# A fused retention and squared-ReLU kernel: q of the first pairs in 2 KB rows, one score task per pair, clusters joined one group earlier, and a re-drawn plan

## The chip, the cores and the metric

The kernel runs on one core of a Trainium2 chip. The time is that of the device for one execution, in microseconds (us); the number to compare is the median of ten executions. One further execution was recorded by the hardware profiler, and everything that is read from a profile comes from that one. The engines are named as in the profile: PE (matmul) with its weight loads PEld, DVE (vector), ACT (scalar), POOL (GpSimd) and SP (the queue that issues most DMAs).

## The reference

```python
scores = (1 / sqrt(D)) * q @ k.T                      # per batch (8) and head (8), 576 positions, D = 64
Dmat[h, i, j] = gamma[h] ** (i - j) if i >= j else 0  # gamma = 1 - 2 ** (-5 - h)
attn = (scores * Dmat) @ v
x = attn with the heads side by side                  # 4608 rows of 512
h = x @ w_in                                          # 512 -> 2048
out = relu(h) ** 2 @ w_out                            # 2048 -> 512
```

Inputs and output are float32; the kernel computes in float16 with float32 sums.

## The kernel before

**Units and groups.** A unit is 128 positions of one batch with all eight heads (or the last 64 positions of two batches, a "tail"). There are 36 units, and two units make a group, 18 groups in all. For each group PE does the retention part in small 64x64 matmuls (four at a time in the corners of the array, the helper `quad`, L357): `psc` are the scores, `psS` the sums of k times v that carry the state on, `psO` the outputs from masked scores and from the state. DVE masks the scores (`rx` L490, `rT` L692), updates the state (`R`, `Rm`, `stmp`) and writes the group's input to the feed-forward part (`xT`, L577 and L751). Then PE does the first product `ph` (L876, 64 matmuls of 128x256 per group), ACT takes the ReLU (`rl`, L884), ACT or DVE the square (`gT`, L894 and L896), and the second product `po` follows: for group 0 directly (L916, 32 matmuls of 128x512), for the others by Strassen's seven products (L973), with sums of `gT` on DVE (`gS`, L946) and differences of `w_out` on DVE (`wT`, L827).

**The first eight units** are loaded in pairs: one DMA each for k, q and v of 256 positions (L316, 512 KB, packets of 512 bytes because two neighbouring positions of one head lie side by side). The casts to float16 are `kx`, `qx` (L424) and `vx` (L420); PE turns k and q around (`psT`, L439), and ACT or DVE copies the turned tiles out (`kqT`, L450). In these four groups the scores are two tasks, one for the even and one for the odd positions (`fs`, L479), each with two banks of PSUM and a lock of its own (`prS`, `prO`). All later units are loaded one by one (k L301, q L298, v L301), cast on POOL (L371, L382, L387) and turned by a DMA (`kqT`, L400).

**Clusters.** A change from the large matmuls to the small ones and back costs PE time, so small tasks are put together. From group JOIN = 5 on, the outputs from the state of group g and the scores of group g+1 are one task (`f1`, L790), and the sums of g+1 and the rest of the outputs of g another (`f2`, L794). Before that, a group's scores and sums are one task (`fa`, L778) and its outputs one with a drain in the middle (`fb`, L809).

**What sets the order.** The program order on every engine comes from a list planner in the kernel (`Schedule`, L16): every task has an engine, a key, an assumed duration and its dependences. `emit` walks through time with these durations and writes the tasks out in the order in which they would start. The assumed durations and the landing delays (`LAG`, `after=`) thus change no instruction, only the order. The queues are in order: what waits at the head of SP or POOL holds up everything behind it.

**The head.** 34 `warm` matmuls (L256) fill PE while the first data come. POOL makes masks and issues the eight casting weight DMAs (w_in 0 to 3 and w_out 0 to 3, L331, numbered w0 to w7 below); the first of them waits for the landing of v of the first pair, and k of the third pair waits for w5 (`behind`). A small constant for the tails (`iota_pt` on POOL L272 and L273, `vdl_tail` on DVE L182, `vdec_tail` on ACT L184) is made here too.

Of the kernel before, what the change touches and what calls it, by code (L numbers as in the profile page):

```python
# [9 lines left out]
FP32 = mybir.dt.float32  # L10
# [5 lines left out]
class Schedule:  # L16
# [7 lines left out]
    def add(self, eng, key, dur, fn, deps=(), acq=(), after=None, lag=0.0):  # L24
        t = dict(eng=eng, key=key, dur=dur, fn=fn, acq=acq, n=len(self.tasks), users=[], free=[], lag=lag,
                 left=len(deps), ready=0.0, lat=self.LAT[eng] if after is None else after)
        for d in deps:
            d["users"].append(t)
        self.tasks.append(t)
        return t  # L30
# [11 lines left out]
    def emit(self):  # L42
# [13 lines left out]
        now = 0.0  # L56
        while True:
            for e in ready:
                if busy[e]:
                    continue  # L60
                held = []
                while ready[e]:
                    item = heapq.heappop(ready[e])
                    t = item[2]
                    if all(self.count[r] >= t["acq"].count(r) for r in t["acq"]):
                        for r in t["acq"]:
                            self.count[r] -= 1
                        t["start"] = now
                        order.append(t)
                        busy[e] = True  # L70
                        push(now + t["dur"], "end", t)
                        break
                    held.append(item)
                for item in held:
                    heapq.heappush(ready[e], item)
            if not events:
                break
            now = events[0][0]
            while events and events[0][0] <= now + 1e-9:
                _, _, what, t = heapq.heappop(events)  # L80
                if what == "end":
                    busy[t["eng"]] = False
                    for w in t["users"]:

                        push(now + (0.0 if w["eng"] == t["eng"] else t["lat"]), "dep", w)
                    for g in t["free"]:
                        push(now + t["lat"], "free", g)
                elif what == "dep":
                    t["left"] -= 1
                    if t["left"] == 0:  # L90
                        push(now + t["lag"], "go", t)
                elif what == "go":
                    heapq.heappush(ready[t["eng"]], (t["key"], t["n"], t))
                else:
                    t["left"] -= 1
                    if t["left"] == 0:
                        self.count[t["res"]] += 1
# [6 lines left out]
def kernel(  # L104
# [9 lines left out]
    nc = tc.nc  # L114
# [96 lines left out]
    mask2 = const.tile([P, 2, 2, 64], FP32, name="mask2")  # L211
    nc.gpsimd.memset(mask2, 1.0)
    for c in range(2):
        for e in range(2):
            m = mask2[c * 64:(c + 1) * 64, e]
            nc.gpsimd.affine_select(out=m, in_=m, compare_op=ALU.is_ge, fill=0.0, base=-e, pattern=[[1, 2], [2, 64]],  # L216
                                    channel_multiplier=-2)
# [12 lines left out]
    BESIDE = 1.1  # L230
# [5 lines left out]
    JOIN = 5  # L236
    LAG = {"k4": 0.7, "q4": 0.5}
# [37 lines left out]
    tail_pool = add_gated("POOL", 4, "v", 2.2, make_tail_pool)  # L275
    tail_dec = add("DVE", 0, 0.3, lambda: make_vdec("tail", tile_of["iota_pt"]), deps=[tail_pool])
# [31 lines left out]
    def add_load_pair(name, u):  # L308
        n = "kqv".index(name)

        def fn():
# [4 lines left out]
            t = nc.sync.dma_start(out=x, in_=(k, q, v)[n][b, :, c * P:(c + 2) * P, :].rearrange("h (p e) d -> p h (e d)", e=2))  # L316
# [3 lines left out]
        loaded[name, u] = loaded[name, u + 1] = dma_task(0, 1.81 if loaded else 2.9, fn, acq=("wst",) if name != "q" else (),  # L320
# [4 lines left out]
    def add_weight(i):  # L325
# [10 lines left out]
        t = add("SP", 0, 2.75, lambda: None, deps=last_load + [issue], after=2.1 + LAG.get(f"w{i}", 0.0))  # L336
# [25 lines left out]
    def half(x):  # L362
        return slice(64 * x, 64 * x + 64)
# [39 lines left out]
    def add_unit_pair(u, base):  # L403
# [4 lines left out]
        for i, name in enumerate("kqv"):  # L408
            xs[name] = []
            for e in range(2):  # L410
                eng = ("DVE" if (e if name == "v" else lead) else "ACT" if name == "k" and u >= 4 or u == 2 and e else
                       "DVE" if name == "q" and u == 2 else "POOL")

                def fc(name=name, e=e, eng=eng):
# [4 lines left out]
                    if name == "v":  # L419
                        (nc.vector if eng == "DVE" else nc.gpsimd).tensor_tensor(  # L420
                            out=t.rearrange("p (h d) -> p h d", d=D), in0=x,
                            in1=vdec[f"pair{e}"].rearrange("p (h o) -> p h o", o=1).to_broadcast([P, H, D]), op=ALU.mult)
                    else:
# [10 lines left out]
        for i, name in enumerate("kq"):  # L434
# [9 lines left out]
            for s in range(2):  # L444
                on_act = i == 0 or s == 0 or u > 0

                def fe(i=i, s=s, on_act=on_act):
                    if i == 0:
                        tile_of["kqT", u + s] = work.tile([P, 2 * NP, P], FP16, name="kqT", tag="kqT", bufs=6)
                    (nc.scalar.copy if on_act else nc.vector.tensor_copy)(  # L450
                        out=tile_of["kqT", u + s][:, i * NP:(i + 1) * NP].rearrange("p x (e t) -> p e x t", e=2),
                        in_=tile_of["psT", u, i][:, :, :, half(s)])
# [15 lines left out]
    def add_ret_pair(g):  # L468
# [7 lines left out]
        for e in range(2):  # L476
            tag = "prS" if e == 0 else "prO"

            def fs(e=e, tag=tag):  # L479
# [6 lines left out]
            t = add("PE", base + 3 + e, 0.4, fs, deps=T["kqT", u] + T["kqT", u + 1], acq=(tag, "kq", "ff", "ff"))  # L486
            ms = []
            for a in range(2):
                def fm(e=e, a=a):
                    nc.vector.tensor_tensor(  # L490
                        out=rT[e][:, a], in0=rT["ps", e][a].rearrange("p (n i) -> p n i", i=P),
                        in1=mask2[:, e].rearrange("p (o e) i -> p o (e i)", o=1).to_broadcast([P, NP, P]), op=ALU.mult)
                ms.append(add("DVE", base + 5 + e, 0.66, fm, deps=[t] + ms))
                sched.free("ff", ms[-1:])
            sched.free(tag, ms)
            masked += ms
# [67 lines left out]
        t = add("PE", base + 23.9, 0.6, fo1, deps=masked + T["kvx", u], acq=("prO", "ff", "ff"))  # L564
# [8 lines left out]
        for s in range(2):  # L573
            def fx(s=s):
                if s == 0:
                    tile_of["x", g] = x_pool.tile([P, NP, 2 * P], FP16, name="xT", tag="xT")
                nc.vector.tensor_tensor(  # L577
                    out=tile_of["x", g][:, :, s * P:(s + 1) * P].rearrange("p n (i e) -> p n e i", e=2),
                    in0=tile_of["psO", g][s].rearrange("p (n e i) -> p n e i", n=NP, e=2),
                    in1=gam_f.rearrange("p n (i e) -> p n e i", e=2), op=ALU.mult)  # L580
            T["x", u + s] = add("DVE", base + 25 + s, 0.7, fx, deps=[t] + ([T["x", u]] if s else []), acq=() if s else ("x",))
            sched.free("ff", [T["x", u + s]])
        sched.free("prO", [T["x", u + 1]])
# [117 lines left out]
    def after_sums(g, t, key, res):  # L701
# [24 lines left out]
        r2 = add("DVE", key + 0.3, 0.65, fr2, deps=[r1], acq=("R",))  # L726
# [95 lines left out]
    def add_wT(i, in0, in1):  # L822
        ts = []
        for h in range(2):
# [3 lines left out]
            ts.append(add("DVE", WT_KEY + i, 0.7, f, deps=sum((wcast[j] for j in range(4, 8 if i else 6)), [])))  # L828
# [6 lines left out]
    for x, y in ((t2, t1), (t4, t2)):  # L835
        for p in y:
            for w in x:
                sched.need(w, p)
# [19 lines left out]
    def add_ff(g):  # L858
# [10 lines left out]
        for fb in range(NF // nf):  # L869
# [18 lines left out]
            def fg(fb=fb, on_act=on_act):  # L888
# [6 lines left out]
                else:  # L895
                    nc.vector.tensor_tensor(out=t, in0=rl, in1=rl, op=ALU.mult)  # L896
            r = add("ACT", place(4 * fb + 4), 0.6, fr, deps=[f1[-1]], acq=("rl",))
            sched.free("ff", [r])
            sq.append(add("ACT" if on_act else "DVE", place(4 * fb + 6), 0.63 if on_act else 0.55, fg, deps=[r] + sq[:1],
                          acq=() if fb else ("g",)))  # L900
# [31 lines left out]
    def add_strassen(g, us, base, sq):  # L932
# [7 lines left out]
        def add_sum(k, key, parts, in0, in1, op, deps, start=()):  # L940
            out_ = []
            for h in range(parts):
# [4 lines left out]
                out_.append(add("DVE", key + h, (BESIDE if h else 0.5) if parts > 1 else 0.8, f, deps=deps(h, parts) + list(start)))  # L947
# [164 lines left out]
```

## Time and profile before

| what | value |
|---|---|
| median of 10 executions (lowest, highest) | 289.84 us (289.27, 290.74) |
| the profiled execution: its own time | 289.79 us |
| its span, from first to last instruction | 288.1 us |
| PE busy | 281.2 us, 98% of the span |
| ACT, DVE, POOL busy | 187.6, 178.1, 87.4 us |
| mean granted PE clock | 1.00 |
| HBM read, written | 36.70 MB, 9.44 MB |

The profiled execution's time is 1.69 us longer than its span. A busy PE is not proof that PE works at its peak, since matmuls overlap; the step from one start to the next tells more. In the timeline the start of a group is in the first column and its length in the second; what ended the idle time before it stands in brackets. The chain of waits follows the last instruction back to what released it.

### The profile page before, as it was taken

The numbers are of one execution on the slowest core, as the hardware profiler recorded it, in microseconds if no ns is written. First come the engines' busy times: TensorE is split into PE (matmuls) and PEld (weight loads), VectorE is DVE, ScalarE is ACT, GpSimd is POOL, SyncE is SP. The second block draws the span as 40 slices with busy tenths as digits, with TensorE's granted clock in tenths as the row PEclk, the third lists the DMA queues.
The fourth block names the chain that finished last, engine by engine and source line by source line (L and its number), as shares of the span: only waits on it lengthen the run. The fifth ranks groups of instructions, "written<-read, shape, count | busy, mean of one in ns | idle before, by whom it ended". The sixth has DMA issues, their size and how long they took to land.

```text
span 288.1 us, 10135 instructions
## 1 busy us (share of the span) xinstructions
PE 281.2 (98%) x4346; PEld 236.1 (82%) x4346; DVE 178.1 (62%) x341; ACT 187.6 (65%) x363; POOL 87.4 (30%) x124
## 2 busy tenths in 40 slices
PE   7999999999999999999999999999999999999994
PEld 2568767888888888888888888888888888888883
DVE  3772389768466756548767574676666566364632
ACT  5558975667584857657576748675848675847830
POOL 5660036443524242434335433362432000000000
PEclk9999999999999999999999999999999999999999
DMA  7999999999999898999999897989989020102004
GB/s 200 276 208 207 248 288 284 149 246 165 224 212 164 221 211 204 193 201 179 226 170 234 193 206 187 251 192 250 163 215 191 0 77 2 73 2 75 0 4 144
DMA packets 122156, 49.94 MB, mean 173 GB/s; under 512 B 94720, under 2 KB 117760, under 8 KB 122112
## 3 DMA queue, kind: packets, MB, share of 16 engines
q1 hardware_dynamic: 117568, 44.84, 71.8%
q0 software_dynamic: 4224, 4.19, 8.8%
q8 instruction: 34, 0.56, 0.8%
q10 hardware_dynamic: 320, 0.26, 0.4%
q14 instruction: 10, 0.08, 0.1%
HBM read 36.70 MB, written 9.44 MB: 160 GB/s over the span
## 4 chain that ended last, share of the span: by engine, by line
PE 89%; DMA 3%; DVE 2%; POOL 2%; issue 2%; DVEq 0%; POOLq 0%
PE ph L876 44%; PE po L973 36%; PE psO L357 4%; DMA w_in<-in_moe_w_in_dram 3%; PE po L916 2%; PE psS L357 2%; PE psc L357 2%; DVE rx L490 1%; DVE o L996 0%; POOL mask L216 0%; DVE gS L946 0%; POOL vx L420 0%; POOL w_in L331 0%; PE psT L439 0%; DVE R L461 0%
## 5 line engine op out<-in xcount | busy, mean ns | idle before, releaser
L876 PE MATMUL ph<-xT,w_in 128*128 128x256 f16 x1152 | 136.6, 273 | 0.1
L876 PEld LDWEIGHTS <-w_in 128*128 128x128 f16 x1152 | 111.4, 98 | 14.5 <-DMA w_in<-in_moe_w_in_dram 0.4
L884 ACT ACTIVATE rl<-ph 128x512 f16<-128x512 f32 x144 | 84.3, 587 | 50.2 <-PE ph L876 47.6
L894 ACT ACTIVATE gT<-rl 128x512 f16<-128x512 f16 x118 | 74.4, 631 | 3.4
L973 PEld LDWEIGHTS <-gS 128*128 128x128 f16 x544 | 51.7, 98 | 6.6 <-DVE gS L946 0.2
L973 PE MATMUL po<-wT,gS 128*128 128x256 f16 x408 | 55.8, 273 | 0.0
L973 PEld LDWEIGHTS <-gT 128*128 128x128 f16 x408 | 39.6, 98 | 4.7
L946 DVE TENSOR_TENSOR gS<-gT,gS 128x512 f16<-128x512 f16 (+1 forms) x51 | 29.9, 586 | 21.1 <-ACT gT L894 20.4
L973 PE MATMUL po<-w_out,gT 128*128 128x256 f16 x272 | 36.7, 273 | 0.0
L387 POOL TENSOR_TENSOR v<-v,vdec_full 128x512 f16<-128x512 f32 x24 | 25.9, 1077 | 18.1 <-DMA v<-in_v_dram 16.1
L371 POOL CAST kq<-k 128x512 f16<-128x512 f32 x28 | 19.6, 699 | 36.0 <-DMA k<-in_k_dram 33.4
L946 DVE TENSOR_TENSOR gS<-gT 128x1024 f16<-128x1024 f16 x34 | 26.1, 768 | 6.5 <-ACT gT L894 6.3
L382 POOL CAST kq<-q 128x512 f16<-128x512 f32 x24 | 16.1, 671 | 36.7 <-DMA q<-in_q_dram 36.5
L896 DVE TENSOR_TENSOR gT<-rl 128x512 f16<-128x512 f16 x26 | 11.8, 453 | 21.2 <-ACT rl L884 21.2
L996 DVE TENSOR_TENSOR o<-po,u 128x256 f32<-128x256 f32 x33 | 13.9, 422 | 15.5 <-PE po L973 7.8
L986 ACT COPY u<-po 128x256 f32<-128x256 f32 x34 | 12.5, 368 | 15.6 <-PE po L973 15.5
L751 DVE TENSOR_TENSOR xT<-psO,gam_full 128x512 f16<-128x512 f32 x28 | 18.0, 685 | 4.2 <-PE psO L357 4.1
L996 DVE TENSOR_TENSOR o<-po,p 128x256 f32<-128x256 f32 x18 | 7.6, 424 | 20.6 <-ACT u L986 12.5
L973 PE MATMUL po<-w_out,gS 128*128 128x256 f16 x136 | 18.0, 273 | 0.0
L692 DVE TENSOR_TENSOR rT<-psc,mask_full 128x512 f16<-128x512 f32 x24 | 15.6, 683 | 3.5 <-PE psc L357 3.2
L973 PE MATMUL po<-wT,gT 128*128 128x256 f16 x136 | 17.6, 273 | 0.0
L461 DVE TENSOR_TENSOR R<-stmp,dec 128x512 f16<-128x512 f32 (+1 forms) x18 | 13.3, 741 | 0.5
(82 smaller groups left out, 221.4 us busy)
## 6 DMA issues: line engine op xcount, KB each, us to landing
out_dram<-o SPq DMA_DIRECT2D x32, 256.0 KB, 2.5
k<-in_k_dram SPq DMA_DIRECT2D x24, 256.0 KB, 4.4
q<-in_q_dram SPq DMA_DIRECT2D x96, 64.0 KB, 3.1
v<-in_v_dram SPq DMA_DIRECT2D x24, 256.0 KB, 3.8
pair<-in_k_dram SPq DMA_DIRECT2D x4, 512.0 KB, 4.2
pair<-in_q_dram SPq DMA_DIRECT2D x4, 512.0 KB, 7.5
pair<-in_v_dram SPq DMA_DIRECT2D x4, 512.0 KB, 7.3
w_in<-in_moe_w_in_dram POOLq DMA_DIRECT2D x4, 512.0 KB, 9.0
```

The costliest lines, as they stand in the source:

```text
L357: t = nc.tensor.matmul(out_, lhsT=lhsT, rhs=rhs, start=start, stop=True, skip_group_check=True, tile_position=(64 * row, 64 * col))
L371: op(out=out_.rearrange("p (n b a d) -> p n b a d", n=2, b=2, a=2), in_=in_.rearrange("p (a n b) d -> p n b a d", n=2, a=2))
L382: nc.gpsimd.tensor_copy(out=tile_of["kq", u][:, 1].rearrange("p (t a d) -> p a t d", t=4, a=2), in_=tile_of["q32", u].rearrange("p (a t) d ...
L387: nc.gpsimd.tensor_tensor(out=t, in0=tile_of["v32", u], in1=vdec[kind].rearrange("p (h o) -> p h o", o=1).to_broadcast([P, H, D]), op=ALU. ...
L692: tile_of["masking", g] = nc.vector.tensor_tensor(out=tile_of["rT", g][:, :, a], in0=tile_of["psc", g][a].rearrange("p (s n i) -> p s n i" ...
L751: nc.vector.tensor_tensor(out=tile_of["x", g].rearrange("p n (s e i) -> p e (n s) i", s=n, e=2)[:, c], in0=y.rearrange("p (o t r) -> p o r ...
L876: nc.tensor.matmul(tile_of["ph", g, fb][:, j, :], lhsT=w_in16[:, m, fi * P:(fi + 1) * P], rhs=tile_of["x", g][:, m, :], start=(m == 0), st ...
L884: nc.scalar.activation(out=t, in_=tile_of["ph", g, fb], func=ACTF.Relu)
L894: nc.scalar.activation(out=t, in_=rl, func=ACTF.Square)
L946: nc.vector.tensor_tensor(out=tile_of["S", g][:, k, sl], in0=in0(sl), in1=in1(sl), op=op)
L973: nc.tensor.matmul(tile_of["pb", g, bank], lhsT=left(i), rhs=right[:, i, :], start=(start and i == 0), stop=(i == HF - 1), skip_group_chec ...
L996: nc.vector.tensor_tensor(out=o_tile(u)[:, half * HM:(half + 1) * HM], in0=bank(x), in1=tile_of[name, g], op=ALU.add)
```

## The change

1. q of a pair comes in two DMAs of 128 rows of 2 KB (eight positions of one head to a row) instead of one of 1024 rows of 512 bytes. The masks (`mask2`), the casts of q, the copies of turned q and the `xT` writes follow the new order of positions.
2. The tail constant is three tasks, on POOL, DVE and ACT, beside the middle of the kernel instead of the head.
3. The scores of a pair are one task with four banks; the locks `prS` and `prO` are gone from the pairs.
4. JOIN is 4.
5. The casts of k and q of the second pair are all on ACT.
6. The planner's figures: landing delays of the early loads, 2.58 for a weight DMA with 3.0 to its landing, durations of some DVE tasks, a model in which some DVE tasks (`soft`) run at 0.22 of their speed while POOL is busy, earlier keys for group 1 (`HURRY`), and a half of `wT` waits only for the weights and the half that it reads.

```diff
-            t = nc.sync.dma_start(out=x, in_=(k, q, v)[n][b, :, c * P:(c + 2) * P, :].rearrange("h (p e) d -> p h (e d)", e=2))
+            src = (k, q, v)[n][b, :, c * P:(c + 2) * P, :]
+            if name == "q":
+                for a in range(2):
+                    t = nc.sync.dma_start(out=x[:, NP * a:NP * a + NP].rearrange("p t d -> p (t d)"),
+                                          in_=src.rearrange("(a x) (r t) d -> a r x (t d)", a=2, t=8)[a])
+            else:
+                t = nc.sync.dma_start(out=x, in_=src.rearrange("h (p e) d -> p h (e d)", e=2))
...
-    mask2 = const.tile([P, 2, 2, 64], FP32, name="mask2")
+    mask2 = const.tile([P, 2, 8, 16], FP32, name="mask2")
...
+                    elif name == "q":
+                        x = tile_of["q32", u].rearrange("p (a t) (s d) -> p a (t s) d", a=2, s=2)[:, :, NP * e:NP * e + NP]
+                        engines[eng](out=t.rearrange("p (t a d) -> p a t d", t=NP, a=2), in_=x)
...
+                    if i == 0:
+                        out_, in_ = out_.rearrange("p x (e t) -> p e x t", e=2), in_[:, :, :, half(s)]
+                    else:
+                        out_ = out_.rearrange("p x (t r) -> p t x r", r=16)
+                        in_ = in_.rearrange("p e y (r x) -> p (e y) x r", x=NP)[:, :, :, 16 * s:16 * s + 16]
...
-                eng = ("DVE" if (e if name == "v" else lead) else "ACT" if name == "k" and u >= 4 or u == 2 and e else
-                       "DVE" if name == "q" and u == 2 else "POOL")
+                eng = ("DVE" if (e if name == "v" else lead) else "ACT" if name == "k" and u >= 4 or u == 2 and name != "v" else "POOL")
...
-        for e in range(2):
-            tag = "prS" if e == 0 else "prO"
-
-            def fs(e=e, tag=tag):
+        def fs():
+            for e in range(2):
                 ps = rT["ps", e] = banks("psc")
...
-            t = add("PE", base + 3 + e, 0.4, fs, deps=T["kqT", u] + T["kqT", u + 1], acq=(tag, "kq", "ff", "ff"))
+        t = add("PE", base + 3, 0.8, fs, deps=T["kqT", u] + T["kqT", u + 1], acq=("kq", "kq", "ff", "ff", "ff", "ff"))
...
-    JOIN = 5
-    LAG = {"k4": 0.7, "q4": 0.5}
+    JOIN = 4
+    LAG = {"k0": 0.3, "q0": 0.6, "v0": 0.3, "k2": 0.2, "q2": 0.5, "v2": 1.0, "w2": 0.7, "w7": 1.4, "k4": 0.3, "q4": 1.1, "v4": 0.9, "q6": 0.8, "v6": 0.2}
...
-    tail_pool = add_gated("POOL", 4, "v", 2.2, make_tail_pool)
-    tail_dec = add("DVE", 0, 0.3, lambda: make_vdec("tail", tile_of["iota_pt"]), deps=[tail_pool])
+    tail_pool = add_gated("POOL", 10, "v", 0.45, make_tail_pool)
+    tail_log = add("DVE", 3 * L, 0.25, make_tail_log, deps=[tail_pool])
+    tail_dec = add("ACT", 3 * L, 0.3, make_tail_dec, deps=[tail_log], after=0.2)
...
-        t = add("SP", 0, 2.75, lambda: None, deps=last_load + [issue], after=2.1 + LAG.get(f"w{i}", 0.0))
+        t = add("SP", 0, 2.58, lambda: None, deps=last_load + [issue], after=3.0 + LAG.get(f"w{i}", 0.0))
...
-            ts.append(add("DVE", WT_KEY + i, 0.7, f, deps=sum((wcast[j] for j in range(4, 8 if i else 6)), [])))
+            ts.append(add("DVE", WT_KEY + i, 0.68, f, deps=wcast[4 + h] + (wcast[6 + h] if i else []), soft=True))
```

Positions of the tasks in the changed program, engine by engine: PE executes the same 4346 matmuls. The 34 warm ones stand in portions of 12, 3, 6, 2, 6, 2, 1, 1, 1 instead of 11, 3, 4, 3, 5, 2, 2, 4. On SP, k and q of unit 8 and k of unit 9 stand ahead of the first and second store, and the two stores of group 1 stand behind k of unit 11.

## Prediction

> **What bounds the kernel now.** I read the page first: busy times and slices.
>
> ```profile
> span 288.1 us, 10135 instructions
> ...
> PE 281.2 (98%) x4346; PEld 236.1 (82%) x4346; DVE 178.1 (62%) x341; ACT 187.6 (65%) x363; POOL 87.4 (30%) x124
> ...
> PE   7999999999999999999999999999999999999994
> ```
>
> PE is busy nearly everywhere, and no other engine passes 65%. To see if this is real work I took the table of windows and the PE timeline, step by step from one matmul's start to the next.
>
> ```profile
> 62.00:260.00 198.00, 197.81 (x3304) 173.04 (x3304) 126.77 (x217) 130.98 (x254) 62.22 (x77) 1.00 0.82 171
> ```
>
> Between 62 and 260 us PE lacks 0.2 us. From the first `ph` at 17.74 to the end the 1152 `ph` and 952 `po` of 256 columns go at 0.109 us a step and the 32 wide `po` at 0.216: 2104 x 0.1092 + 32 x 0.216 = 236.7 us that no order can change. The last PE step ends at 283.96, so 266.2 - 236.7 = 29.5 us is small matmuls, transposes and changes between them, and only one plain wait is in it: w1, below. So time can be won in three places: before the first `ph`, in that wait, and in the clusters of small matmuls. What follows the last matmul (to 288.1) keeps its instructions.
>
> The head, from the timeline and, last two lines, the chain of waits:
>
> ```profile
> 5.88 0.76 DVE L424 CAST kx<-pair 128x512 f16<-128x512 f32 x2
> 6.36 0.73 PE L439 MATMUL psT<-ident,kx 128*128 128x128 f16 x8 [0.31 <-DVE kx L424]
> ...
> 17.74 3.51 PE L876 MATMUL ph<-xT,w_in 128*128 128x256 f16 x28
> ...
> 19.76 1.21 PEld L876 LDWEIGHTS <-w_in 128*128 128x128 f16 x12 [0.38 <-DMA w_in<-in_moe_w_in_dram]
> ```
>
> ```profile
> 11.02 8.71 DMA w_in<-in_moe_w_in_dram
> 19.77 1.49 PE ph L876 x12
> ```
>
> The chain goes through the landing of w1 (19.72), not through the 17.74: PE starts on w0, then waits 0.38 us for w1. The semaphore updates give the landings: k0 5.06, q0 6.86, v0 8.66, k2 10.47, q2 12.29, v2 14.01, w0 17.29, w1 19.72, w2 22.22, w3 24.88, w4 27.42, w5 30.47, w6 32.56, w7 35.41. It is one string: 1.8 us a pair load, about 2.6 us a weight, with the DMA engines full.
>
> **The change, part by part.**
>
> *q in 2 KB rows.* A pair load is 1024 packets of 512 B, 64 on each of 16 engines at 32 ns: 1.8 us by the landings. 2 KB packets to SBUF do not occur; the nearest row is the stores, whose 2 KB packets take a median 84 ns (mean 90 to 101 beside other traffic), against 4 x 32 = 128 ns for the same bytes. That gives 16 x 90 = 1.4 us, 0.4 to 0.45 saved for each q; bounds zero (if the time goes by bytes) and 0.6 (84/128 of 1.8). Two q loads stand ahead of w1: it lands 0.9 earlier at best; 0.4 if w0 follows only its issue, which waits for v0 (issue 8.96) and so for one q; nothing if rows do not matter. I take 0.6: w1 at 19.1. The cut in two adds one SP issue per pair (a q issue took 0.56 us at the start); the string hides it.
>
> The Trainium skill, "DMA: Bandwidth & Descriptors", Specifications, says that 512 B already suffices for line rate, and its Rules for kernel authors say that two transfers to disjoint partition halves are not worth it against one; by these the gain here would be zero. The trace's 512 B packets move 251 to 267 GB/s and its 2 KB ones 325 to 364, so I weigh the row higher.
>
> *Does PE follow?* The changed order on PE, with the durations above: 12 warm end where kx now ends a wait (6.36), so the earlier kx (DVE no longer waits until 5.75 for the tail constant, k0 landed 5.06) gives nothing there. psT k, 3 warm, psT q end at 8.03 as before; 6 warm to 9.4; psc to 10.2; psS waits for POOL's vx (w0 issue 0.99 after v0 at 8.2, then 1.04): 10.65 to 11.05; 2 warm; psT of k2 at 11.5 (k2 at 10.0, two ACT casts of 0.62), 6 warm, psT of q2 at 13.25; 2 warm; psO (1.07) to 15.2; 1 warm; psc (0.72; its kqT is ready at 15.0) to 16.2; psS 0.4; 1 warm: first `ph` at 17.0 instead of 17.74, with xT at 16.6 and w0 at about 16.7. 16 `ph` take 1.75, so PE meets w1 at 18.75 and waits 0.35. After 32 `ph` and psO it stands at 19.15 + 1.75 + 1.09 = 22.0; before, the same work (28 `ph`, psO, 4 `ph`) ended at 22.7. Start: 0.7 won. But in the new order 92 `ph` and not 100 stand ahead of the po that needs w5: PE comes there at 29.4 and w5, shifted by 0.6, lands at 29.9. Before, PE came at 31.0 with w5 at 30.47. This leaves 31.0 - 0.87 - 29.9 = 0.2, or 0.7 if w5 follows w4 by the usual 2.55 and not by 3.05. **I take 0.45**, bounds 0 and 0.9.
>
> *The copies of turned q* get a stride of four in PSUM, which no row shows: bounds 425 ns (DVE, L450) and 0.69 (the DVE tasks that read float32 from PSUM); ACT's copies took 586 to 603 in the shapes that occur. The 0.26 between falls only on one copy ahead of psc, and PE waits for POOL's vx there. Casts of q: shape of L382, 0.67 against 0.69 on POOL. `xT` with a strided read: L751 has such a read and takes 685. All zero. The casts of the second pair add 2 x 0.62 to ACT, idle there since 8.81, and take 0.42 and 0.63 from DVE and POOL.
>
> *Tail constant*: 0.41 on POOL, 0.23 on DVE, 0.30 on ACT move to about 60 us, where DVE and ACT have a third free; its reader is group 8. Zero; 0.3 if an `rl` stood on the path.
>
> *One score task per pair.* By start times on PE, the small clusters of groups 2 and 3 (without psT) now last 0.38 + 0.57 + 1.36 + 0.62 + 0.52 + 1.09 = 4.54 (psS 43.05, psc 44.19, psO with half a psc 47.51, psS 49.19, second half 50.57, psO 55.56). Whole tasks: psc 0.57 to 0.72, psS 0.38, psO 1.07, psS 0.38, psc 0.57 to 0.72, psO 1.09: 4.06 to 4.36. **0.35 won**; bounds 0 (the waits inside come back as waits for DVE's masks) and 0.48. Four banks of eight at once is a new constraint; PE's other tasks then have four.
>
> *JOIN 4.* From the chain of waits:
>
> ```profile
> 62.06 0.38 PE psc L357 x32
> 62.44 0.29 PE psS L357 x32
> ...
> 67.64 0.24 PE psO L357 x8
> 67.88 0.09 issue
> 67.96 0.57 PE psO L357 x39
> ...
> 85.57 0.25 PE psO L357 x16
> 85.82 0.26 PE psc L357 x32
> ...
> 89.67 0.38 PE psS L357 x32
> 90.05 0.40 PE psO L357 x48
> ```
>
> Groups 4 and 5 pay 0.67 (scores, sums), 0.89 (outputs, with the drain) and 0.66 (76.94, scores of 5). Joined, as at 85.57 and 89.67, it is 0.67 + 0.51 + 0.78. **0.26 won**, rounded 0.3, and this one hangs on nothing but the order. The whole order has 39 clusters instead of 40.
>
> The plan's figures and the `wT` dependences add no instruction; they show only in the order.
>
> **Sum:** 0.45 + 0.35 + 0.3 = 1.1; 289.79 - 1.1 = **288.7 us**. The profiled execution is 0.05 under the median, so I use it as it stands. All bounds at their best: 0.9 + 0.48 + 0.3 = 1.7, 288.1. If this holds: 288.1 to 289.2.
>
> **Rivals.**
>
> *A: the loads do not keep up with the earlier scores (slower).* With JOIN 4 the scores of group 5 come 80 large matmuls behind those of group 4 and not 112: at 61.25 + 0.67 + 8.8 = 70.75, where they were at 76.94. They need the transpose of unit 11:
>
> ```profile
> 67.35 1.48 SPq L400 DMA_TRANSPOSE kqT<-kq  x1
> ```
>
> It landed at 72.39. If SP is not earlier, PE stands 1.65 us; if k of unit 9, which now waits for an earlier landing on SP's ring of eight, is 1 us later still, 2.65. Then 288.7 + 1.65 to 2.65 = 290.4 to 291.4. Against it: k of unit 8 was issued at 42.15 behind a store that waited for ACT, and is now ahead of it, at 39.8 by v of unit 6 (40.35, released by POOL's qx, which comes 0.95 earlier); 25.2 us of issues later this puts the transpose at 65.0 and its landing at 70.0. The slack is 0.7. It decides from a landing later than 72.4.
>
> *B: rows do not matter and the gain at the start is lost*, because w1 and w5 land when they did: 0.3 + 0.35 = 0.65, and if the score task's banks make PE wait as well, 0.3 alone: 289.1 to 289.5.
>
> *C: the order merely deals the waits anew*, PE meeting k4, q4 and vx just before 50 us (each computed with 0.1 to 0.4 us of slack) and losing 1.1 there: 289.8, no change.
>
> **Chances.** Below 0.2% (0.58 us) a measurement of this kernel can hardly tell from no change. Forecast 0.58; the better half of B (289.1 to 289.2) 0.10; its rest and C, 289.3 to 290.4, 0.15; A 0.17. Faster 0.68, same 0.15, slower 0.17. Range 287.9 to 290.4: the forecast's bounds with 0.2 for the spread between executions, and up to the foot of A.
>
> **What would show it.** First `ph` near 17.0; w1 near 19.1 (if 19.7, rows do not matter); PE idle before the po of w5 under 0.5; clusters of groups 2 and 3 summing to 4.1 to 4.4 and the two joined ones of group 4 to 0.51 and 0.78; no wait of PE for a transpose near 70. Wrong if PE's timeline has a gap of over 0.5 us behind 20 us.

## The result and the profile after

The changed kernel is **slower**: a median of 291.36 us (289.63 to 293.34, 15 executions) against 289.77 us for the kernel before (289.27 to 290.74, 51 executions). The ratio is 1.0057, with a 95% interval of 1.0045 to 1.0069. It also varies more: its executions spread over 3.7 us, those before over 1.5 (beside the experiments below, in 19 to 30 executions each, over 2.1 to 5.2). Ratios leave out executions more than 1.5% above the fastest of their kernel (one of twelve in e1, three of twelve in e13, two of thirty of the kernel before beside e9 to e12), while medians and spreads leave out none.

The profiled execution took 292.53 us, so it is one of the long ones. From its page, busy times and slices (PEclk is the granted PE clock in tenths):

```profile
span 290.8 us, 10142 instructions
...
PE 282.2 (97%) x4346; PEld 237.4 (82%) x4346; DVE 177.3 (61%) x340; ACT 188.5 (65%) x365; POOL 87.1 (30%) x123
...
PE   8999999969999999999999999999999999999994
...
PEclk9999999997999999999999999999999999999999
```

PE still dominates, but its ninth slice (58 to 65 us) has fallen to 6, and in the tenth the clock is at 7. The table of windows (start and end, length, PE, PEld, DVE, ACT and POOL busy, clock, DMA share, GB/s) shows it finer:

```profile
62.00:260.00 198.00, 195.45 (x3210) 170.12 (x3209) 124.12 (x216) 130.23 (x253) 63.02 (x78) 0.99 0.83 171
...
64.00:66.00 2.00, 1.01 (x7) 0.75 (x7) 1.30 (x3) 1.97 (x5) 0.00 (x0) 0.81 0.97 109
66.00:68.00 2.00, 2.00 (x11) 1.44 (x10) 1.90 (x5) 0.58 (x2) 0.62 (x1) 0.50 1.10 239
68.00:70.00 2.00, 2.00 (x17) 1.67 (x16) 2.00 (x4) 1.68 (x4) 1.10 (x1) 0.83 1.33 207
```

Between 62 and 260 us PE now lacks 2.55 us where it lacked 0.2, and behind the hole the clock is at half for 3.41 us. The timeline names what PE stood behind:

```profile
58.06 0.78 SPq L337 DMA_DIRECT2D v<-in_v_dram  x1
...
61.67 1.04 POOL L429 TENSOR_TENSOR v<-v,vdec_full 128x512 f16<-128x512 f32 x1 [1.24 <-DMA v<-in_v_dram]
...
62.93 0.23 POOL L300 TENSOR_SCALAR iota_pt<-iota_p 64x1 f32<-64x1 f32 x1
63.19 0.67 DVE L304 TENSOR_SCALAR vdl_tail<-lnrow,iota_pt 128x8 f32<-128x8 f32 x1 [3.50 <-POOL iota_pt L300]
...
63.89 0.30 ACT L308 ACTIVATE vdec_tail<-vdl_tail,lnscale 128x8 f32<-128x8 f32 x1 [3.50 <-DVE vdl_tail L304]
...
64.98 0.78 PE L1015 MATMUL po<-wT,gS 128*128 128x256 f16 x4 [2.45 <-ACT p L1028]
```

Read from the top: the load of v of unit 10 lands at 61.60; POOL's cast waited for it, the tail constant's `iota_pt` stood behind that cast, DVE and then ACT stood 3.50 us each behind the constant, and PE 2.45 us behind ACT. So the tail constant, which I had costed at nothing, is the visible stop of this execution. Its 2.7 us on PE, and some 1.7 us lost to the half clock after it (PE steps of 0.213 us where 0.109 is usual), are more than the 2.7 us by which the span grew. But it is not the cause of the slower median, as the first experiments show: of sixteen executions, the profiled one among them, five have a mean clock of 0.993 or 0.994 and lie at 292.5 to 293.3; the other eleven kept 0.998 to 1.0 and still a median of 291.1.

The early part went as forecast. The first `ph`, in the timeline, and then the joined clusters of group 4 in the chain of waits:

```profile
17.34 2.67 PE L918 MATMUL ph<-xT,w_in 128*128 128x256 f16 x23
```

```profile
74.91 0.26 PE psc L399 x28
...
80.08 0.38 PE psS L399 x32
80.45 0.38 PE psO L399 x37
```

By the semaphore updates w1 lands at 18.83 (19.72 before) and w5 at 29.09 (30.47), and PE waits for neither. To see where time was won and lost along the way I took one more reading of PE's timeline, its own time: the start of each group's scores on PE, less the large matmuls that stand ahead of them (0.1092 us each, 0.216 for the wide `po`). What is left is the time that went into small clusters, changes and waits, in us (last row: start of the last PE step):

| up to | before | after | tail in head (e2) | without stores (e8) | old load figures (e14) |
|---|---|---|---|---|---|
| scores of group 4 | 26.25 | 25.08 | 25.74 | 25.53 | 25.48 |
| group 5 | 28.02 | 30.18 | 26.57 | 26.36 | 26.31 |
| group 6 | 28.94 | 31.74 | 28.12 | 27.91 | 27.86 |
| group 10 | 34.54 | 37.33 | 34.96 | 33.51 | 33.48 |
| group 12 | 37.58 | 40.48 | 38.19 | 36.55 | 36.51 |
| last PE step | 47.02 | 49.78 | 48.14 | 45.85 | 46.50 |

At the scores of group 4 the changed kernel is 1.17 us ahead. It then loses 4.0 us on the way to group 6, and nothing more.

### The profile page after: what moved, and what is told of

It is laid out like the page before. It is cut to its first block, busy times and chain, and to the rows that moved or that the text cites. A ratio compares the mean times of both kernels' runs of the same rounds, so it can differ in the third digit from the quotient of the medians.

```text
span 290.8 us, 10142 instructions
## 1 busy us (share of the span) xinstructions
PE 282.2 (97%) x4346; PEld 237.4 (82%) x4346; DVE 177.3 (61%) x340; ACT 188.5 (65%) x365; POOL 87.1 (30%) x123
## 4 chain that ended last, share of the span: by engine, by line
PE 87%; POOL 3%; DMA 3%; SPq 2%; issue 2%; ACT 1%; DVE 1%; POOLq 0%; DVEq 0%
PE ph L918 42%; PE po L1015 34%; PE psO L399 4%; PE po L958 2%; PE psS L399 2%; PE psc L399 2%; DMA k<-in_k_dram 2%; SPq L442 1%; DMA v<-in_v_dram 1%; PE warm L283 1%; PE psT L483 1%; SPq L334 1%; SPq L337 1%; POOL mask L243 1%; ACT kqT L500 0%
## 5 line engine op out<-in xcount | busy, mean ns | idle before, releaser
L918 PE MATMUL ph<-xT,w_in 128*128 128x256 f16 x1152 | 138.4, 275 | 0.0
L988 DVE TENSOR_TENSOR gS<-gT,gS 128x512 f16<-128x512 f16 (+1 forms) x51 | 30.9, 607 | 20.3 <-ACT gT L936 19.7
L988 DVE TENSOR_TENSOR gS<-gT 128x1024 f16<-128x1024 f16 x34 | 24.9, 732 | 9.5 <-ACT gT L936 9.4
L413 POOL CAST kq<-k 128x512 f16<-128x512 f32 x28 | 20.5, 734 | 29.9 <-DMA k<-in_k_dram 28.3
L938 DVE TENSOR_TENSOR gT<-rl 128x512 f16<-128x512 f16 x26 | 11.0, 423 | 14.8 <-ACT rl L926 14.6
L509 DVE TENSOR_TENSOR R<-stmp,dec 128x512 f16<-128x512 f32 (+1 forms) x18 | 14.1, 782 | 0.5
```

The source lines that it names most:

```text
L413: op(out=out_.rearrange("p (n b a d) -> p n b a d", n=2, b=2, a=2), in_=in_.rearrange("p (a n b) d -> p n b a d", n=2, a=2))
L918: nc.tensor.matmul(tile_of["ph", g, fb][:, j, :], lhsT=w_in16[:, m, fi * P:(fi + 1) * P], rhs=tile_of["x", g][:, m, :], start=(m == 0), st ...
L988: nc.vector.tensor_tensor(out=tile_of["S", g][:, k, sl], in0=in0(sl), in1=in1(sl), op=op)
```

## The experiments

"Before" is run on the same chip beside each; ratios are to it. Theory 1: the tail constant's wait is the cause.

**e1, e2: the constant later, or in the head; e3: work in the hole; e4: the constant alone.** e1 and e2 keep the changed order and move only the constant's tasks (e2's edit below; in e1 they go 80 tasks further back). e3 puts eleven matmuls of 512 columns ahead of the first `ph` of group 3. e4 is the kernel before with part 2 of the change alone.

```diff
+        head = [t for t in order if "move" in t]
+        order[:] = head + [t for t in order if "move" not in t]
```

```diff
+                        if (g, fb) == (3, 0):
+                            for _ in range(11):
+                                nc.tensor.matmul(tile_of["ph", g, fb].rearrange("p j c -> p (j c)"), lhsT=w_out16[:, 0, 0:P],
+                                                 rhs=w_out16[:, 0, :], start=True, stop=True)
```

> The changed kernel with the same order of all instructions, except that the two last steps of the tail constant (vdl_tail on DVE, vdec_tail on ACT) stand later on their engines, 18 ACT instructions further on; nothing is left out. Theory 1 (ACT, in order, is held by vdec_tail, which waits over DVE for POOL's iota_pt, which stands behind POOL's v cast of unit 10, whose data landed at 61.60 us): PE's wait of 2.45 us at 65.0 us and the half clock of 3.41 us after it both go; from the profiled 292.5 us 2.6 and 1.5 us are taken off, 288.4 us, up to 288.9 if PE now meets the transpose of unit 11 (landed 70.69) before it is there; fewer differences between executions. Rival (the loads are late, and PE would have waited for them anyway): the wait moves to the scores of group 5 near 70 us and the time stays at 290.5 or more.

> The changed kernel with all three steps of the tail constant at the head of POOL, DVE and ACT, as before the change; every other instruction keeps its place. Theory 1: as with the late constant, within 0.2 us of it, since twelve warm matmuls hide the later kx (5.9 instead of 5.1 us): 288.4 to 288.9. Rival (the head gains from the constant's leaving it): 0.4 to 0.7 us slower than with the late constant, with the first ph that much later. If the loads are the cause of the wait: 290.5 or more.

> The changed kernel with eleven more matmuls of 512 columns (w_out times w_out into the bank that the first ph of group 3 then overwrites) just ahead of the wait; 11 x 0.216 = 2.4 us of PE work in the 2.45 us for which PE stands. Theory 1 with a clock part (the idle time costs itself, and a fall of the granted clock to half for 3.4 us in some executions costs 1.5 us more): the wait is as long, filled, the granted clock stays at 1.00, the executions above 292 us vanish, median about 290.5 to 291.0 against 291.4. If the fall of the clock has nothing to do with the idle time: the clock still falls at 65 us in some executions, and the median stays at 291.4 or more.

> The kernel before with the tail constant alone in three steps (POOL behind the v cast of unit 10, DVE and ACT where the plan puts them); the plan moves some ph between 70 and 90 us with it. Theory 1 (the cost lies in where ACT's step stands against POOL's): here vdec_tail stands behind the first u copy of group 3, at about 65.5 us by the profile of before, and POOL's cast of v of unit 10 ended at 64.1 and iota_pt would at 64.7, so ACT waits little: 289.6 to 290.1, no change. Rival (the three steps cost wherever they stand, by the engines' changes between tasks or because nobody can hide them): 291 or more, as in the changed kernel.

Measured: e1 291.75 us, ratio 1.0042 (1.0017 to 1.0066); e2 291.45, 1.0049 (1.0022 to 1.0076); e3 291.76, 1.0064 (1.0038 to 1.0089); e4 290.03, 0.9998 (0.9985 to 1.0011). **Theory 1 fell.** Without the stop and without the fall of the clock the kernel is as slow as with them. PE's waits in e2 say where the time is then:

```profile
PE psc L402 <- DMA kqT<-kq: 0.9, 2, 0.6
```

```profile
83.06 0.32 PE L402 MATMUL psc<-kqT 64*64 64x64 f16 x16 [0.55 <-DMA kqT<-kq]
...
121.82 0.32 PE L402 MATMUL psc<-kqT 64*64 64x64 f16 x16 [0.31 <-DMA kqT<-kq]
```

The scores now wait for turned k and q (0.55 us of idle PE before 83.06, 0.31 before 121.82; four such waits, 1.6 us, in e1). The stop had only hidden this: it gave the transposes the time that they needed. e3 says the same from the other side: 2.4 us of added PE work (11 x 0.216) make the ratio 1.0064 in place of 1.0057, some 0.2 us (the intervals overlap).

Slack is the time from a transpose's landing to the start of the scores that read it (negative where they had to wait). For the later unit of groups 5, 6, 7, 8 and 9 it was 4.5, 2.6, 2.9, 3.5 and 3.5 us before; in e2 it is 0.1, -0.8, 0.0, 0.1 and -0.6.

**e5 to e8: JOIN, the rows, the supply.** Theory 2 is the prediction's rival A: the supply of turned k and q doesn't keep up, because of JOIN. Theory 3 is that the new head does the harm. e7 puts the loads, masks, casts and copies of before into e2; e8 leaves stores out:

```diff
-    JOIN = 4
+    JOIN = 5
```

```diff
+        if u < 16:
+            return
```

> The changed kernel with the tail constant in the head, and JOIN 5 instead of 4 (the order is planned anew; up to the outputs of group 4 PE's order is that of the kernel with JOIN 4). Theory 2 (supply): what the change wins at the start and in the clusters is lost again where PE reaches the scores of groups 5 to 10 before the turned k and q have landed; the transposes are no earlier than before, since their stream on SP and the DMA engines has a pace of its own. With JOIN 5 the scores of group 5 come about 6 us later and are covered again (slack 2.4 to 3.5 us as before, less the 0.8 to 1.2 us won): no wait for kqT over 0.4 us at groups 5 to 9, 288.9 to 289.5 us, and a spread as narrow as before's. Theory 3 (the head): the 2 KB rows and the new head themselves make the time longer and the spread wide, JOIN has no part in it: 291 to 291.7, spread of 3 us.

> The kernel before with JOIN 4 alone (planned anew from the outputs of group 4 on). Theory 2 (supply): PE reaches the scores of group 5 some 6 us earlier and waits there and at groups 6 to 8 for the transposes; 290.4 to 291.4, with kqT waits of 0.4 us and more in the PE timeline. Theory 3 (the head): nothing of the head is touched, the joined clusters win 0.3: 289.8.

> The changed kernel with the tail constant in the head, and q of a pair again in one DMA of 512-byte rows, with the masks, casts and copies that belong to it; the order on every engine is the same. Theory 2 (supply): PE's start is later by 0.4 to 0.9 us, and the waits for the transposes at groups 5 to 10 shrink by as much: 291.2 to 291.8, no change against the same kernel with 2 KB rows, spread still 3 us. Theory 3 (the head): the rows are what made it slow: 290.0, narrow.

> The changed kernel with the tail constant in the head, and without the stores of units 0 to 15 (that half of the output is left out); the order of everything else is the same. Theory 2 (supply): SP and the DMA engines are relieved of 4 MB before 150 us, the transposes of groups 5 to 10 land 1 us or more earlier, the waits for kqT go, and 288.7 to 289.6 us with a narrow spread come out, since the stores themselves are on no path of PE. Theory 3 (the head): the stores come after the head: 291.4, spread 3 us.

Measured: e5 291.06 us, 1.0028 (1.0007 to 1.0048); e6 290.47, 1.0001 (0.998 to 1.0023); e7 293.35, 1.0115 (1.0086 to 1.0143), four executions; e8 288.32, 0.9936 (0.9914 to 0.9958). e8 settles that supply is the place: its PE waits for no transpose, its spread is 0.7 us (four executions), and its own-time column lies 0.7 to 1.7 us ahead of before all the way. But JOIN by itself is not the reason (e5 stays slow; e6's interval takes in 1, though its median is 0.5 us above that of before), and theory 3 is out: the 2 KB rows *save* 1.9 us in this order (e7 against e2). I had expected no change from e7; four pair loads, each 0.4 us shorter, move the supply (in e7's trace the transposes of units 11, 13, 15, 17 and 19 land 0.4 to 1.6 us later than in e2's), and here PE follows the supply.

**e9 to e12: the planner's figures.** What had moved the scores? Before, 488, 592, 700 and 808 large matmuls stand ahead of the scores of groups 6 to 9 in the trace; after, 464, 576, 680 and 776: 16 to 32 fewer, 1.7 to 3.5 us, most of the slack of before (2.6 to 3.5). The plan's own times say why: with the change's figures for the early loads it has the transpose of unit 10 at 61.05 us and of unit 16 at 99.45, where it had 65.21 and 102.41. On the chip SP did not follow. SP's transposes of units 10, 12 and 14, before and then after (start, length of the issue):

```profile
63.62 2.85 SPq L400 DMA_TRANSPOSE kqT<-kq  x1
...
75.56 1.67 SPq L400 DMA_TRANSPOSE kqT<-kq  x1
...
87.52 2.73 SPq L400 DMA_TRANSPOSE kqT<-kq  x1
```

```profile
63.28 1.62 SPq L442 DMA_TRANSPOSE kqT<-kq  x1
...
74.55 2.57 SPq L442 DMA_TRANSPOSE kqT<-kq  x1
...
87.50 2.93 SPq L442 DMA_TRANSPOSE kqT<-kq  x1
```

They are 0 to 1 us earlier and not 3 to 4 (in e2 0 to 1.8 us later than before). Before, the plan was 0.7 to 1.6 us late against the chip (units 10 to 16), which was its safety; after, it is 1.0 to 3.1 us early. Theory 4: these figures are the cause. e9 and e10 give it the safety back in another figure (e10 5.5, with JOIN 5), e11 puts the figures alone into the kernel before, e12 takes the stores of e8 from the kernel before, as a control:

```diff
-        T["kqT", u] = [add("SP", -1, 2.4, fx2, deps=[ck, cq], acq=("kqT",), after=3.0, lag=LAG_T)]
+        T["kqT", u] = [add("SP", -1, 2.4, fx2, deps=[ck, cq], acq=("kqT",), after=6.5, lag=LAG_T)]
```

> The changed kernel with the tail constant in the head, and one figure of the planner changed: the time it assumes from the end of a transpose's issue to its landing is 6.5 instead of 3.0 (no instruction changes, only the order: the scores of groups 5 to 9 are planned at 74.9, 86.0, 99.4, 112.3 and 124.9 us, where the kernel before has 77.4, 86.0, 99.0, 112.3 and 125.4 and the changed one 71.6, 82.9, 96.7, 109.6 and 121.4). Theory 4 (the plan's figures): the change's weight and q figures make the planner believe that the transposes are issued 3 to 4 us earlier than in the plan of before (61.05 against 65.21 for unit 10, 99.45 against 102.41 for unit 16), while on the chip they are not earlier by more than 1 us; so it puts the scores 16 to 32 large matmuls further forward, and the slack of 2.6 to 3.5 us is gone. Expected: the slack is back above 1.5 us at groups 5 to 9, no wait for kqT, 288.6 to 289.3 us, spread below 1.5 us. Theory 2 (supply, with JOIN as the cause): 290.5 to 291.5.

> The changed kernel with the tail constant in the head, JOIN 5, and 5.5 for the planner's landing of a transpose (scores of groups 5 to 9 planned at 77.0, 85.3, 98.2, 112.0 and 125.1 us, as in the plan of before). What is left of the change is the 2 KB rows and the one score task, with the clusters of before. Theory 4 (the plan's figures): 288.7 to 289.3, narrow; beside e9 it prices JOIN 4 by itself (0.3 less for e9 if the joined clusters are free). Theory 2: 289.5 to 290.5.

> The kernel before with the change's figures for the early loads alone (the landing delays LAG, 2.58 and 3.0 for a weight DMA, 1.41 for q of a pair, which here still comes in 512-byte rows); no instruction changes, only the planned order (transposes planned at 61.05, 73.45, 86.05, 98.25 us instead of 65.21, 76.41, 89.01, 102.41; scores of groups 6 to 9 at 82.8, 96.6, 108.6 and 122.2 instead of 86.0, 99.0, 112.3 and 125.4). Theory 4 (the plan's figures): the kernel before becomes as slow as the changed one or slower, 291 to 293 us with a wide spread, and waits for kqT at groups 6 to 9. Theory 2 with JOIN as the cause: 289.8, as before.

> The kernel before without the stores of units 0 to 15 (that half of the output is left out), order otherwise the same: the control for the run without stores. Theories 2 and 4 alike: the kernel before has slack at its transposes, so relief changes nothing, 289.5 to 290.0; then the 3.1 us that the changed kernel wins by it are waits on the supply, and what is left of the difference, 1.2 to 1.6 us, is what the change is worth where the supply keeps up. If it falls to 288.3 as well, the kernel before is bound by the supply too and the change has won nothing.

Measured: e9 290.65 us, 1.0018 (0.9997 to 1.0039); e10 289.65, 0.999 (0.9976 to 1.0003), spread 1.4 us; e11 **296.03**, 1.0208 (1.0184 to 1.0231); e12 289.83, 0.999 (0.9975 to 1.0005). e11 is the clearest run of the study: no instruction of the kernel before is changed, only figures that the planner assumes, and it loses 6 us. PE's waits, then two groups of its timeline:

```profile
PE psc L357 <- DMA kqT<-kq: 4.3, 3, 2.4
```

```profile
84.69 0.32 PE L357 MATMUL psc<-kqT 64*64 64x64 f16 x16 [0.34 <-DMA kqT<-kq]
87.39 0.32 PE L357 MATMUL psc<-kqT 64*64 64x64 f16 x16 [2.38 <-DMA kqT<-kq]
```

The scores of group 6, unit by unit, each wait for their own transpose. But the earlier place of the scores is only part of it. SP's transposes of units 10, 12 and 14 in e11:

```profile
68.19 1.24 SPq L400 DMA_TRANSPOSE kqT<-kq  x1
...
79.79 2.76 SPq L400 DMA_TRANSPOSE kqT<-kq  x1
...
92.69 2.82 SPq L400 DMA_TRANSPOSE kqT<-kq  x1
```

They are issued 4.2 to 5.2 us later than before: the figures re-draw SP's order as well as PE's (k and q of unit 8 stand ahead of the first store, as in the changed program), and PE itself is 2.0 us late at the scores of group 4 (64.01 us, 61.99 before). That e11 loses more than the changed kernel may be due to its q in 512-byte rows, for which the figure for q is wrong too; e7 has the same mismatch and loses 1.15%, e11 2.08%, so this isn't shown. e12 shows that before had little to gain from lighter traffic (0.1%), so most of the 3 us of e8 are waits that the change brought. e9 and e10 mend part of it, and both stay above what I had expected of them. In e9 the scores of groups 6 to 9 stand behind 480, 588, 692 and 796 large matmuls, nearly as before, yet the later unit's transposes land 1.2 to 2.9 us later than before, and the slack is still -0.3 to 0.8 us; its trace has a wait of 0.9 us for a transpose, at group 10. How much of the loss is the scores' earlier place and how much the later transposes, no run separates.

**e13 to e16: what limits the supply, and what the rest is worth.** e14 undoes the load figures in e2 and nothing else:

```diff
-    LAG = {"k0": 0.3, "q0": 0.6, "v0": 0.3, "k2": 0.2, "q2": 0.5, "v2": 1.0, "w2": 0.7, "w7": 1.4, "k4": 0.3, "q4": 1.1, "v4": 0.9, "q6": 0.8, "v6": 0.2}
+    LAG = {"k4": 0.7, "q4": 0.5}
...
-        t = add("SP", 0, 2.58, lambda: None, deps=last_load + [issue], after=3.0 + LAG.get(f"w{i}", 0.0))
+        t = add("SP", 0, 2.75, lambda: None, deps=last_load + [issue], after=2.1 + LAG.get(f"w{i}", 0.0))
...
-dma_task(0, 2.9 if not loaded else 1.41 if name == "q" else 1.81, fn,
+dma_task(0, 1.81 if loaded else 2.9, fn,
```

e13 (from e2) and e16 (from e10) send the stores of the first 16 units by ACT's queue:

```diff
+        if u < 16:
+            engs = (nc.scalar, nc.scalar)
```

> The changed kernel with the tail constant in the head, its plan as it is, and the stores of units 0 to 15 issued on ACT's queue instead of SP's, at the same places of the order. Theory 5 (SP's issues are the limit: each takes 0.4 to 0.6 us and SP issues nearly without a pause from 56 to 96 us): transposes 1 to 2 us earlier, no wait for kqT, 288.4 to 289.3 us. Theory 6 (the transfers themselves are the limit): 291 to 291.8 as with SP. A third outcome, ACT held up by the stores' waits: rl late, gaps of PE at po, over 291.

> The changed kernel with the tail constant in the head and the figures of before for the early loads (2.75 and 2.1 for a weight, 1.81 for each pair load, LAG of k4 and q4 alone); parts 1, 3, 4 and 5 stay, and the rest of part 6. Transposes planned as in the plan of before (65.21, 76.41, 89.01, 102.41 us), scores of groups 5 to 9 at 74.5, 85.9, 98.4, 112.2 and 126.6. Theory 4 (the plan's figures): 288.6 to 289.4 us, spread below 1.5 us, no wait for kqT over 0.4. If the rest of the change is worth nothing: 289.8 to 290.2.

> As the kernel with the figures of before, and JOIN 5 again (scores of groups 5 to 9 planned at 77.7, 86.2, 98.9, 111.8 and 124.5 us): of the change only the 2 KB rows and the one score task are left. Theory 4: 0.3 slower than with JOIN 4 if the joined clusters are free (288.9 to 289.6); if JOIN 4 brings scores ahead of their transposes, faster than with JOIN 4.

> The kernel with JOIN 5 and the later landing (289.65 us), with the stores of units 0 to 15 on ACT's queue. Theory 5 (SP's issues): supply has slack to spare, all waits left go: 288.6 to 289.2. Theory 6 (transfers): 289.6.

Measured: e13 290.89 us, 1.0007 (0.9979 to 1.0035), from 288.32 to 293.86; e14 **289.41**, 0.9982 (0.9969 to 0.9995); e15 289.45, 0.9981 (0.9967 to 0.9995); e16 291.75, 1.0084 (1.0051 to 1.0117). e14 beats both kernels. Its span, from the page, and its window:

```profile
span 287.6 us, 10139 instructions
```

```profile
62.00:260.00 198.00, 197.83 (x3243) 172.61 (x3242) 127.38 (x216) 131.06 (x253) 62.60 (x76) 1.00 0.81 171
```

PE lacks 0.2 us again, and none of its waits is for a transpose; the plan is 0.9 to 2.7 us late against the chip (units 10, 12, 14 and 16), and slack at groups 5 to 9 is 4.1, 2.0, 1.3, 1.4 and 3.2 us. So the load figures cost 0.67%, 1.9 us (1.0049 against 0.9982). e15 prices JOIN 4 in this plan: nothing (289.41 against 289.45). With the load figures JOIN 4 was the slower both times (e2 1.0049 against e5 1.0028, e9 1.0018 against e10 0.999), by 0.2 to 0.3%, hardly more than the noise (e9 and e10 also differ in the landing figure). On theory 5 against 6 the answer is mixed. In e13 SP issues the transposes of units 13 and 14 earlier than in e2 (76.61 and 86.69, where e2 has 78.5 and 89.3), but they take 6.9 and 6.5 us to land, where e2's took 4.5, and ACT holds up PE in another place:

```profile
PE psc L402 <- DMA kqT<-kq: 1.5, 1, 1.5
...
PE po L1020 <- ACT u L1033: 1.0, 1, 1.0
```

The Trainium skill, "DMA: Bandwidth & Descriptors", Issuing engines are not separate DMA queues, says that transfers issued from different engines run on the same 16 DMA engines and interleave. The longer landings in e13 fit that. In e16 PE waits for no transpose, but the scores wait 0.9 us for ACT's `rl`; at 1.0084 it is worse than e10. Which share of the supply's limit is issue on SP and which is transfer is not settled.

**e17, e18: what is left.** e14 won 0.5 us where I had forecast 1.1. e17 undoes the DVE figures too; e18 takes the stores from e14:

```diff
-add("DVE", key + h - HURRY * (g == 1), 0.43 if parts > 1 else 0.72, f, deps=deps(h, parts) + list(start), soft=True)
+add("DVE", key + h - HURRY * (g == 1), (BESIDE if h else 0.5) if parts > 1 else 0.8, f, deps=deps(h, parts) + list(start))
```

> As the kernel with the figures of before for the loads and JOIN 4, with the DVE figures of before too (gS 0.5, 1.1 and 0.8 instead of 0.43 and 0.72, gT 0.55 instead of 0.43, R 0.65, wT 0.7, no soft model, no HURRY): all of part 6 but the finer wT dependences is undone. If the DVE figures cost the late 0.5 us: 288.8 to 289.0. If not: 289.3 to 289.5.

> As the kernel with the figures of before for the loads and JOIN 4, without the stores of units 0 to 15 (that half of the output is left out). If what is left of the loss is supply: 288.3, as the changed plan without stores. If it is the DVE figures or the head: 289.2 to 289.4, as the kernel before, which won only 0.1 to 0.3 by it.

Measured: e17 290.18 us, 1.0003 (0.9984 to 1.0022); e18 288.14, 0.9936 (0.9916 to 0.9956). The DVE figures are not what is missing; if anything they help (e17's trace has new waits of 1.1 us for POOL's `vx` and 0.9 for `xT`). Lighter traffic wins another 1.3 us in e18: relieved of the stores, the change is worth 0.54%, 1.6 us give or take 0.7 (0.9936 against e12's 0.999), in keeping with the forecast of 1.1. Which wait this removes is not shown, since e14's trace has none for a transpose.

## Why the prediction was wrong

**The step that failed** is the sentence "The plan's figures and the `wT` dependences add no instruction; they show only in the order." Both halves are true, and I priced the order at nothing. The load figures alone cost 1.9 us in the changed kernel and 6 us in the kernel before: with them the slack of 2.6 to 4.5 us between the transposes' landings and the scores that read them was gone (-0.8 to 0.1 in e2). I worked out PE's own order to 30 us and the slack of one transpose, that of unit 11; I did not count the large matmuls ahead of the scores of groups 6 to 9, which the changed program gave before any run.

Rival A had the mechanism, scores ahead of their loads, but not the cause: it charged JOIN and group 5, while every group from 5 to 9 was moved to the edge, and with the old load figures JOIN 4 costs nothing. Its price (290.4 to 291.4; measured 291.36) is therefore luck. Its chance of 0.17 rested on "The slack is 0.7" for one unit; and the scores of group 5 stood 120 large matmuls behind those of group 4 in the trace of before, not 112.

The other steps, by their measures:

- *Start, 0.45, and one score task, 0.35.* At the scores of group 4 the trace of after is 1.17 us ahead of before. Over ten traces with the changed head the own time there is 25.08 to 27.09, 25.73 on average; over four with the head of before (before, e4, e6, e12) it is 26.12 to 27.00, average 26.49. That is 0.76 won, 0.8 forecast: right on average, though single traces of the two sets overlap. The small clusters of groups 2 and 3 sum to 4.05 us in the trace of after (4.54 before; 4.06 to 4.36 forecast). How it splits is less clear: in the trace of after the first `ph` came at 17.34 (17.0 forecast) and w1 at 18.83 (19.1), but over the ten traces at 17.81 and 19.19 on average, and before at 17.74 and 19.72.
- *q in 2 KB rows* was given to PE's start alone. The saving on each q was sized right, 0.4 us: in the second pair q landed 1.82 us behind k before and 1.41 after (the working beside it is loose, since 64 packets at 32 ns would be 2.05 us and not 1.8). It also shortens the supply, and in a plan that is tied to the supply it is worth 1.9 us (e7). The Trainium skill, "DMA: Bandwidth & Descriptors", by whose Specifications 512 bytes suffice, would have it at nothing; the measurement decides for the rows. The rule on partition halves that the prediction names does not bear on it, since each of the two DMAs writes all 128 partitions.
- *Tail constant, zero.* Wrong in the profiled execution (a 2.45 us wait), nothing in the median (e2). It is the same fault in another dress: the plan had `iota_pt` at 60.85 us, behind a load that landed later than it assumed.
- *JOIN 4, 0.3.* The clusters are as forecast (0.66 + 0.50 + 0.76 = 1.92 us by starts, 2.22 before), but the time doesn't show it (e14 against e15), so this term of the sum was not won.
- *The sum*, 1.1, was sound for PE as far as this shows: with lighter traffic it is 1.6, give or take 0.7. "Wrong if PE's timeline has a gap of over 0.5 us behind 20 us" was the right alarm.

## What to carry to other kernels

Where a list planner writes the order, a changed cost figure is a change of the program: count, from the changed order, how much of the bound engine's work stands ahead of each operation that needs a transfer, and set it against that transfer's slack in the trace. A figure that was wrong on the safe side may be what keeps a kernel fast; making one figure truer takes the margin from under another that is not (e11). And a long wait in one trace is not the cause of a slower median until a run without it is faster: here it was removed and the next limit took its place.

## What the runs showed of the hardware

A single gap of 2.73 us between two PE starts was followed by 3.41 us of half clock (0.50 from 65.26 to 68.67 us), and 256-column matmuls took 213 ns a step where 109 is usual. The Trainium skill, "TensorE: Matmul & The Clock Gate", Why this matters for your kernels, warns of gaps above about 3 us; this one was shorter. It did not fall each time: eleven of sixteen executions of this program had a mean clock of 0.998 or more (whether PE stood as long in them is not on record). With the constant moved or the hole filled (e1 to e3), all thirty executions had 0.997 or more. With the changed head the first `ph` lay anywhere from 17.3 to 18.4 us over the ten traces, and the first loads landed up to 1.2 us apart (q0 at 6.52 in after and 7.69 in e1). That this spread reaches the end where the plan is tied to the supply, while the kernel before, with 2.6 to 4.5 us of slack, kept within 1.5 us in the 51 executions of the result, fits those runs; no run isolates it, and beside the experiments that kernel too spread over 2.1 us and more.
